# The tanh of the second MoE's up projection goes to a PSUM bank, half a block at a time

## Chip, cores and metric

One NeuronCore of a Trainium2 chip runs the whole program. The metric is device time in microseconds (us), the median of three runs; lower is better.

## What is computed

```python
kv = einsum('bhsd,bhse->bhde', k, v); out = einsum('bhsd,bhde->bhse', q, kv)      # 8 x 8 heads, 576 x 64
x  = out / sqrt(mean(out*out, -1) + 1e-06) * g_norm                               # 4608 tokens x 512
h  = x @ w_in;   x = maximum(0.01 * h, h) @ w_out                                 # first MoE, d_ff 2048
h  = x @ w_in2;  out = (h - tanh(h)) @ w_out2                                     # second MoE, d_ff 2048
```

All inputs and the output are float32; the weights are read as raw 64-bit words and converted on the chip. The line that matters here is the last one: `h - tanh(h)`.

## The kernel before

After the attention the program has four phases, one for each weight matrix. In the trace of before, phase three (the second up projection with `h - tanh(h)`) runs on TensorE from 823.85 to 1158.70 us, and phase four (the second down projection) from there to the end.

**Blocks and products.** Phase three has 72 blocks: 9 superblocks of 512 tokens by 8 pieces of d_ff. A block is a 2 x 2 matrix of 128 x 256 tiles and is computed with seven products instead of eight (Strassen's scheme); every product is six fp16 matmuls of 128 x 256 (high and low halves of the operands). `up` (line 748) issues the products in *rounds* of seven in the order of `ORDER2`: 1 of block n, 7 and 5 of block n-1, 3 of block n-2, 6 of block n, 4 of block n-1, 2 of block n. Products 1, 6, 7, 4 of a block add up in one PSUM bank (`ps_a`), and between them ScalarE copies the bank out (`keep`, line 698): `c` after product 1, `u` after 6, `u` after 7, and the block's tile 21 (`g`) after 4. Product 6 of a block must wait for its `c`, 7 for the first `u`, 4 for the second: TensorE waits there if ScalarE is late. Products 2, 5 and 3 go to banks `ps_b` and `ps_c`, and VectorE adds them to `c` and `u` (`add`, line 707) into the 128 x 1024 tile `g`.

**The activation.** When product 3 of a block is done, `finish` starts a chain of steps: ScalarE takes the tanh of the whole `g` (128 x 1024) into a tile `th` of the pool of 21 large SBUF places (line 1428), VectorE subtracts it in two halves of 128 x 512 (line 1432), and a DMA stores `g`, which phase four reads later.

**What else runs beside it in phase three.** VectorE and ScalarE convert the last weight matrix (lines 432 to 456; later lines 518 and 521) and split the next superblock's input (lines 578 and 585, with sums on GpSimd, line 616). From about 1100 us on they make the operands of phase four (`gl`).

**What sets the order.** Nothing is scheduled on the chip. `Plan` lays all instructions on one time axis with fixed costs per step (the first numbers in the tuples, in us) and emits them in that order; each engine then runs its own instructions strictly in that order and waits on semaphores. A chain puts each step at the first gap of its engine, where a last number in a tuple allows it to overlap its successor by so much; a step that raises `NoRoom` is tried again 0.4 us later. `bank(n, ...)` marks a PSUM bank as used until `free(n)`.

**Banks.** In phase three `banks2` gives `ps_a` banks 0, 1, 4, `ps_b` 2 and 5, `ps_c` 3 and 6, so bank 7 stands idle. In phase four `ps_d`, the target of product 4, has bank 4 for one half of the tokens and bank 7 for the other.

Of the kernel before, what the change touches and what calls it, by code (L numbers as in the profile page):

```python
# [11 lines left out]
F32 = mybir.dt.float32  # L12
I32 = mybir.dt.int32
AF = mybir.ActivationFunctionType
ALU = mybir.AluOpType
# [15 lines left out]
P = 128  # L31
# [172 lines left out]
@with_exitstack  # L204
def body(ctx, tc, *args):
    q, out, w1 = args[0], args[-1], args[4]
    sizes = (*q.shape, *out.shape, w1.shape[1])
    pools = {
        "const": ctx.enter_context(tc.tile_pool(name="const", bufs=1)),
        "wpool": ctx.enter_context(tc.tile_pool(name="wpool", bufs=1)),  # L210
        "work": ctx.enter_context(tc.tile_pool(name="work", bufs=1)),
        "dram": ctx.enter_context(tc.tile_pool(name="dram", bufs=1, space=DRAM)),
        "ps": ctx.enter_context(tc.tile_pool(name="ps", bufs=1, space=PSUM)),
    }
    delays = {}
    unseen = Unseen()
    while True:
        late = lay_out(Plan(delays, True), unseen, {n: unseen for n in pools}, sizes, [unseen] * len(args))
        if late is None:
            break  # L220
        delays[late[0]] = delays.get(late[0], 0.0) + late[1]
    with tc.manual_schedule():
        lay_out(Plan(delays, False), tc.nc, pools, sizes, args)


def lay_out(plan, nc, pools, sizes, args):
    q, k, v, g_norm, w1, w2, w3, w4, out = args
# [6 lines left out]
    T2 = 256  # L234
# [8 lines left out]
    L, M, X = (Slots(plan, work, kind, n) for kind, n in (("l", NL), ("m", NM), ("x", NX)))  # L243
    at = plan.at

    used = set()

    def bank(n, name):
        if n in used:
            plan.miss(("bank", n))  # L250
        used.add(n)
        return ps.tile([P, 512], F32, tag=f"p{n}", name=name)

    def free(n):
        used.discard(n)
        plan.met(("bank", n))
# [902 lines left out]
    t = 1.0  # L1159
# [7 lines left out]
    for o in order:  # L1167
        if o[0] == "a":
            held = {}
# [52 lines left out]
    for hp in range(4):  # L1222
        c = PAIRS[hp]
        t_, held = ta[0, c]
# [16 lines left out]
    for b in range(1, B):  # L1241
        for hp in range(4):
# [4 lines left out]
            held = ta[b, c][1] if (b, c) in ta else {}  # L1247
# [172 lines left out]
    spread(lambda i, kk, t: split_late(2, i, kk, t, L, M), UNITS, end1 + 45.0, end2 - 28.0)  # L1420


    def tanh(g, s):
        held = {}

        def one():
            held["t"] = L.take([P, 4, T2], F32, "th", True)
            nc.scalar.activation(out=held["t"].ap, in_=g(), func=AF.Tanh)  # L1428

        def two(n):  # L1430
            o = g()[:, 2 * n:2 * n + 2]
            nc.vector.tensor_tensor(out=o, in0=o, in1=held["t"].ap[:, 2 * n:2 * n + 2], op=ALU.subtract)  # L1432

        return [
            ("A", 1.15, one),
            ("V", 0.7, lambda: two(0)), ("V", 0.7, lambda: two(1)),
            (None, 0.0, lambda: L.give(held["t"])),
        ]

    def banks2(n):  # L1440
# [7 lines left out]

    state["rest"] = second_scales(whole, NS2, end2 + 12.0)
    up(1, T2, NS2, x1ops, tanh, lambda s: consts[s][1:3], banks2, ORDER2, between2, freed_to(3, 0.4))  # L1450
    end3 = plan.pe
    c3 = end2 + 0.45 * (end3 - end2)
# [77 lines left out]
```

## Time and profile before

| | |
|---|---|
| median of 3 runs | 1490.52 us (1490.04 to 1491.99) |
| profiled execution, its own time | 1495.29 us |
| its span (first to last instruction) | 1493.5 us |
| granted TensorE clock, mean | 0.986 of full speed (1.00 throughout phases two to four) |
| busy: TensorE, VectorE, ScalarE, GpSimd | 97%, 83%, 63%, 40% of the span |

The profiled execution is 4.8 us longer than the median, of which 1.8 us lie outside its span. TensorE is busy nearly throughout, so what matters is not the busy share of another engine but the places where TensorE waits for one.

### The profile page before, as it was taken

Reading aid. Unit: us, or ns where it says so; the run is one execution under the profiler, and the core shown is the slowest. Engines: PE = TensorE matmul, PEld = TensorE weight load, DVE = VectorE, ACT = ScalarE, POOL = GpSimd, SP = SyncE. Lnnn points to the kernel's source line nnn. Section 1 sums busy time; section 2 is a strip of 40 time slices with the busy share of each in tenths; the row PEclk is TensorE's granted clock in tenths of the full one; section 3 lists DMA queues with packets and bytes.
Section 4 is the critical chain, followed back from the end, with each engine's and each line's share of the span. In section 5 each row is a group of like instructions: output and inputs, shape, how many; then the busy total and the mean of one; then the engine's idle time right before and its main releaser. Section 6 shows DMA issues by size and latency. Waiting matters only on the chain. (4 is left out here: it accounts for less than half of the span.)

```text
span 1493.5 us, 32922 instructions
## 1 busy us (share of the span) xinstructions
PE 1443.8 (97%) x12674; PEld 1195.8 (80%) x12674; DVE 1245.4 (83%) x2029; ACT 933.7 (63%) x1529; POOL 599.8 (40%) x614
## 2 busy tenths in 40 slices
PE   5699999999999999999999999999999999999998
PEld 3467777767777777777777888888888888888887
DVE  4896687677877899999996999989999998888871
ACT  5587777778877644444542677768888555555540
POOL 3141340453643444445542111126577444444430
PEclk8799999999999999999999999999999999999999
DMA  9737898899978745555555856646678744444421
GB/s 281 182 105 228 267 298 263 275 327 306 335 260 300 296 166 191 173 173 200 178 172 198 307 211 221 209 172 221 250 253 320 282 143 154 142 143 146 150 86 36
DMA packets 156461, 321.83 MB, mean 215 GB/s; under 512 B 16656, under 2 KB 98448, under 8 KB 156304
## 3 DMA queue, kind: packets, MB, share of 16 engines
q1 hardware_dynamic: 156304, 319.73, 64.7%
q8 instruction: 99, 1.62, 0.4%
q14 instruction: 58, 0.48, 0.1%
HBM read 189.66 MB, written 130.01 MB: 214 GB/s over the span
## 5 line engine op out<-in xcount | busy, mean ns | idle before, releaser
L639 PEld LDWEIGHTS <-w 128*128 128x128 f16 x8400 | 820.1, 98 | 198.1 <-issue 19.2
L616 POOL TENSOR_TENSOR gl<-gl 128x256 f32<-128x256 f32 (+1 forms) x288 | 322.9, 1122 | 368.3 <-DVE gl L616 132.4
L639 PE MATMUL ps_a<-ops,w 128*128 128x288 f16 (+1 forms) x2400 | 331.7, 282 | 6.5 <-ACT c L696 2.8
L639 PE MATMUL ps_c<-ops,w 128*128 128x288 f16 (+1 forms) x2352 | 314.7, 282 | 2.4 <-DVE g L707 2.3
L639 PE MATMUL ps_a<-opa,w 128*128 128x288 f16 (+1 forms) x2016 | 284.6, 281 | 5.6 <-DVE w L521 4.1
L639 PEld LDWEIGHTS <-ops 128*128 128x128 f16 x1728 | 169.1, 98 | 20.0 <-issue 0.4
L639 PE MATMUL ps_b<-opa,w 128*128 128x288 f16 (+1 forms) x1200 | 175.5, 283 | 0.2 <-DVE r_w L344 0.2
L616 DVE TENSOR_TENSOR gl<-gl 128x288 f32<-128x288 f32 (+1 forms) x256 | 142.4, 558 | 4.3
L616 POOL TENSOR_TENSOR x1g<-x1g 128x256 f32<-128x256 f32 x72 | 69.5, 966 | 172.0 <-PE ps_a L639 109.9
L639 PEld LDWEIGHTS <-opa 128*128 128x128 f16 x1296 | 126.8, 98 | 14.7
L576 ACT ACTIVATE ops<-gl 128x1152 f16<-128x1152 f32 x64 | 74.3, 1161 | 96.2 <-POOL gl L616 96.0
L585 DVE SCALAR_TENSOR_TENSOR ops<-gl,inv,ops 128x1024 f16<-128x1024 f32 x72 | 104.3, 1450 | 28.1 <-ACT ops L578 28.0
L578 ACT ACTIVATE ops<-gl,inv 128x1024 f16<-128x1024 f32 x72 | 82.3, 1144 | 65.7 <-POOL gl L616 65.7
L1432 DVE TENSOR_TENSOR g<-g,th 128x512 f32<-128x512 f32 x144 | 111.9, 787 | 0.9 <-ACT th L1428 0.9
L698 ACT ACTIVATE u<-ps_a,up 128x256 f32<-128x256 f32 x144 | 68.1, 473 | 55.0 <-PE ps_a L639 51.3
L583 DVE TENSOR_TENSOR ops<-gl,ops 128x1152 f16<-128x1152 f32 x64 | 94.2, 1475 | 6.9 <-ACT ops L576 6.9
L707 DVE SCALAR_TENSOR_TENSOR g<-ps_c,u 128x288 f32<-128x288 f32 x128 | 57.9, 452 | 49.2 <-PE ps_c L639 48.5
L639 PE MATMUL ps_c<-w,ops 128*128 128x256 f16 x864 | 97.3, 273 | 0.2 <-DVE osb L707 0.2
L639 PE MATMUL ps_a<-w,ops 128*128 128x256 f16 x864 | 95.8, 273 | 0.0
L1079 POOL TENSOR_TENSOR xg<-xg,bc 128x288 f32<-128x288 f32 x48 | 44.8, 961 | 123.8 <-DMA bc<-iv 55.1
L583 DVE TENSOR_TENSOR opa<-gl,opa 128x864 f16<-128x864 f32 x64 | 81.0, 1266 | 2.0 <-ACT opa L576 1.6
L585 DVE SCALAR_TENSOR_TENSOR opa<-gl,inv,opa 128x768 f16<-128x768 f32 x72 | 79.6, 1106 | 0.8 <-ACT opa L578 0.8
(133 smaller groups left out, 2062.3 us busy)
## 6 DMA issues: line engine op xcount, KB each, us to landing
g<-g SPq DMA_DIRECT2D x64, 576.0 KB, 5.1
gl<-g SPq DMA_DIRECT2D x64, 576.0 KB, 4.5
g<-g SPq DMA_DIRECT2D x72, 512.0 KB, 3.4
gl<-g SPq DMA_DIRECT2D x72, 512.0 KB, 4.2
wd<-wo SPq DMA_DIRECT2D x48, 448.0 KB, 3.4
w<-wd SPq DMA_DIRECT2D x24, 896.0 KB, 8.5
words<-in_moe_w_in_dram SPq DMA_DIRECT2D x64, 256.0 KB, 7.1
words<-in_moe_w_out_dram SPq DMA_DIRECT2D x64, 256.0 KB, 4.5
```

The lines of the kernel that those rows point to most:

```text
L576: nc.scalar.activation(out=o, in_=i_, func=AF.Copy)
L578: nc.scalar.activation(out=o, in_=i_, func=AF.Identity, scale=scale())
L583: nc.vector.tensor_tensor(out=o, in0=i_, in1=h, op=ALU.subtract)
L585: nc.vector.scalar_tensor_tensor(out=o, in0=i_, scalar=scale(), in1=h, op0=ALU.mult, op1=ALU.subtract)
L616: lambda: e.tensor_tensor(out=g()[:, o], in0=g()[:, a], in1=g()[:, b], op=op),
L639: nc.tensor.matmul(out=out_, lhsT=a, rhs=c, start=start and m == 0, stop=stop and m == n - 1, skip_group_check=not fresh,)
L698: nc.scalar.activation(out=t, in_=src, func=AF.Identity, scale=self.scale)
L707: nc.vector.scalar_tensor_tensor(out=o, in0=src, scalar=self.minus if sub else self.scale, in1=t, op0=ALU.mult, op1=ALU.add,)
L1079: e.tensor_tensor(out=x, in0=x, in1=held[kk].ap[:, n0:n1], op=ALU.mult)
L1432: nc.vector.tensor_tensor(out=o, in0=o, in1=held["t"].ap[:, 2 * n:2 * n + 2], op=ALU.subtract)
```

## The change

The tanh is taken half a block at a time into PSUM bank 7 (a bank holds just 128 x 512 float32), and VectorE subtracts it from there. The second half can only be written once the first has been subtracted, since there is one such bank for the whole phase; so can the first half of the next block. The large SBUF place for `th` is gone.

```diff
+    TANH = 7
+
     def tanh(g, s):
         held = {}
 
-        def one():
-            held["t"] = L.take([P, 4, T2], F32, "th", True)
-            nc.scalar.activation(out=held["t"].ap, in_=g(), func=AF.Tanh)
+        def one(n):
+            if TANH in used:
+                raise NoRoom("bank")
+            held[n] = bank(TANH, "th")[:, :2 * T2].rearrange("p (o t) -> p o t", o=2)
+            nc.scalar.activation(out=held[n], in_=g()[:, 2 * n:2 * n + 2], func=AF.Tanh)
 
         def two(n):
             o = g()[:, 2 * n:2 * n + 2]
-            nc.vector.tensor_tensor(out=o, in0=o, in1=held["t"].ap[:, 2 * n:2 * n + 2], op=ALU.subtract)
+            nc.vector.tensor_tensor(out=o, in0=o, in1=held[n], op=ALU.subtract)
+            free(TANH)
 
         return [
-            ("A", 1.15, one),
-            ("V", 0.7, lambda: two(0)), ("V", 0.7, lambda: two(1)),
-            (None, 0.0, lambda: L.give(held["t"])),
+            step for n in range(2)
+            for step in (("A", 0.65, lambda n=n: one(n), 0.5), ("V", 0.65, lambda n=n: two(n), 0.4))
         ]
```

The lines after it move down by four (1436 is the subtraction now, 1432 the tanh). Because the steps cost the plan something else, the order around them changes too. TensorE's order stays the same but for two tiny matmuls of a weight's scale.

**ScalarE, one round in the middle of phase three** (the round that begins at 922.69 us in the trace of before; `c1`, `u3`, `u2`, `g` are the copies out of `ps_a` after products 1, 7, 6, 4, `unit` is a weight conversion). Before:

```order
L698 ACTIVATE c1_12352<-ps_a_12335,up0_10543 128x256 [waits PE_49]
L698 ACTIVATE u3_12367<-ps_a_12271,up0_10543 128x256 [waits PE_49]
L432 ACTIVATE unit_12379<-words_12190 128x512 [waits DMAHW6_49,DMAHW5_49]
L698 ACTIVATE u2_12395<-ps_a_12335,up0_10543 128x256 [waits PE_49]
L698 ACTIVATE g_12342<-ps_a_12271,up0_10543 128x256 [waits PE_49]
L1428 ACTIVATE th_12407<-g_12278 128x1024 [waits DVE_49,Activation_49]
```

and now:

```order
L1432 ACTIVATE th_12369<-g_12245 128x512 [waits DVE_49]
L698 ACTIVATE c1_12387<-ps_a_12371,up0_10543 128x256 [waits PE_49]
L1432 ACTIVATE th_12402<-g_12178 128x512 [waits DVE_49]
L698 ACTIVATE u3_12404<-ps_a_12302,up0_10543 128x256 [waits PE_49]
L432 ACTIVATE unit_12417<-words_12221 128x512 [waits DMAHW5_49,DMAHW4_49]
L1432 ACTIVATE th_12433<-g_12245 128x512 [waits DVE_49]
L698 ACTIVATE u2_12435<-ps_a_12371,up0_10543 128x256 [waits PE_49]
L698 ACTIVATE g_12378<-ps_a_12302,up0_10543 128x256 [waits PE_49]
```

The tanh stood behind the four copies of its round; now one half stands ahead of `u3` and one ahead of `u2`, and both wait for VectorE.

**VectorE, the same round, now** (`ps_b` and `ps_c` rows are the additions of line 707; a row that reads `th` is the subtraction):

```order
L707 SCALAR_TENSOR_TENSOR g_12378<-ps_b_12361,up0_10543,c1_12320 128x256 [waits DMAHW4_49,PE_49]
L456 SCALAR_TENSOR_TENSOR unit_12235<-words_12031,unit_12235 128x512 [waits DVE_49]
L1436 TENSOR_TENSOR g_12245<-g_12245,th_12369 128x512 [waits Activation_49]
L707 SCALAR_TENSOR_TENSOR g_12378<-ps_c_12395,up0_10543,u3_12404 128x256 [waits PE_49,Activation_49]
L707 SCALAR_TENSOR_TENSOR g_12309<-ps_c_12323,up0_10543,u2_12291 128x256 [waits PE_49]
L1436 TENSOR_TENSOR g_12178<-g_12178,th_12402 128x512
L436 TENSOR_SCALAR unit_12417,mw_325<-unit_12417 128x512 [waits Activation_49]
```

The half `th_12369` is subtracted behind a weight conversion, and `th_12402` behind the two additions of this round, the first of which needs `u3_12404`.

**VectorE at the passage from phase three to phase four, now** (the last additions of phase three, then operands of phase four, `ops`, `opa`, `gl`):

```order
L585 SCALAR_TENSOR_TENSOR ops_16013<-gl_15763,inv0_10540,ops_16013 128x1024 [waits DMAHW2_49,Pool_49]
L1436 TENSOR_TENSOR g_15877<-g_15877,th_16045 128x512 [waits Activation_49]
L707 SCALAR_TENSOR_TENSOR g_16021<-ps_c_16026,up7_11125,u2_15998 128x256 [waits PE_49]
L585 SCALAR_TENSOR_TENSOR opa_16041<-gl_15927,inv0_10540,opa_16041 128x768 [waits DMAHW0_49]
L1436 TENSOR_TENSOR g_15952<-g_15952,th_16064 128x512 [waits Activation_49]
L616 TENSOR_TENSOR gl_15927<-gl_15927 128x256 [waits DVE_49]
```

The fourth matmul into `ps_d`, the first one into bank 7, has a new wait on VectorE: for the subtraction of `th_16064`. The last three halves no longer stand here. They come some 25 VectorE instructions later, behind the two additions that read `ps_d` in phase four's first superblock, once bank 7 is free again.

## Rows read from the trace of the kernel before

**Rows 1.** The page: busy time and share of the span, instructions, of each engine.

```profile
PE 1443.8 (97%) x12674; PEld 1195.8 (80%) x12674; DVE 1245.4 (83%) x2029; ACT 933.7 (63%) x1529; POOL 599.8 (40%) x614
```

**Rows 2.** Waits of TensorE in phase three: us in total, times, longest.

```profile
PE ps_c L639 <- DVE g L707: 1.9, 2, 1.5
PE ps_a L639 <- ACT c L698: 0.6, 1, 0.6
PE ps_a L639 <- DVE r_w L344: 0.5, 1, 0.5
```

**Rows 3.** Groups of phase three by shape: names, shapes, count | busy us, mean ns | idle before.

```profile
L1432 DVE TENSOR_TENSOR g<-g,th 128x512 f32<-128x512 f32 x144 | 111.9, 787 | 0.9 <-ACT th L1428 0.9
...
L1428 ACT ACTIVATE th<-g 128x1024 f32<-128x1024 f32 x72 | 75.3, 1048 | 1.5 <-DVE g L707 1.4
...
L707 DVE SCALAR_TENSOR_TENSOR g<-ps_c,up,u 128x256 f32<-128x256 f32 x144 | 65.9, 477 | 13.2 <-PE ps_c L639 9.8
...
L456 DVE SCALAR_TENSOR_TENSOR unit<-words,unit 128x512 int32<-128x512 int32 x13 | 8.8, 680 | 0.0
...
L432 ACT ACTIVATE unit<-words 128x512 f32<-128x512 f32 x13 | 8.7, 670 | 0.0
...
L616 DVE TENSOR_TENSOR gl<-gl 128x256 f32<-128x256 f32 x3 | 1.2, 410 | 0.0
...
L711 DVE TENSOR_TENSOR xst<-u,ps_d 128x288 f32<-128x288 f32 x2 | 0.9, 444 | 0.0
```

**Rows 4.** The tile `th`, the subtractions: ns min/median/max.

```profile
L1432 DVE TENSOR_TENSOR g<-g,th x144: 669/684/1268, 839.5 to 1169.6; 128x512 f32<-128x512 f32 x144
```

**Rows 5.** Timeline: VectorE beside GpSimd: start us, us, engine, line, op.

```profile
906.33 3.86 POOL L616 TENSOR_TENSOR x1g<-x1g 128x256 f32<-128x256 f32 x4 [1.20 <-ACT u L698]
906.46 1.21 DVE L1432 TENSOR_TENSOR g<-g,th 128x512 f32<-128x512 f32 x1
...
907.59 0.86 DVE L707 SCALAR_TENSOR_TENSOR g<-ps_c,up,u 128x256 f32<-128x256 f32 x2
```

**Rows 6.** Timeline: one round of phase three, from product 1 on.

```profile
922.69 0.82 PE L639 MATMUL ps_a<-opa,w 128*128 128x256 f16 x6
922.89 0.48 DVE L707 SCALAR_TENSOR_TENSOR g<-ps_b,up,c 128x256 f32<-128x256 f32 x1
...
924.20 0.47 ACT L698 ACTIVATE u<-ps_a,up 128x256 f32<-128x256 f32 x1 [0.18 <-PE ps_a L639]
...
924.93 1.07 DVE L707 SCALAR_TENSOR_TENSOR g<-ps_c,up,u 128x256 f32<-128x256 f32 x2 [0.35 <-PE ps_c L639]
925.31 0.82 PE L639 MATMUL ps_a<-ops,w 128*128 128x256 f16 x6
...
925.97 0.82 PE L639 MATMUL ps_a<-opa,w 128*128 128x256 f16 x6
926.17 0.47 ACT L698 ACTIVATE u<-ps_a,up 128x256 f32<-128x256 f32 x1 [0.93 <-PE ps_a L639]
...
927.93 0.82 PE L639 MATMUL ps_a<-ops,w 128*128 128x256 f16 x6
```

**Rows 7.** Windows late in phase three: us, busy (x) of each engine, PEclk, DMA, GB/s.

```profile
1100.00:1135.00 35.00, 35.00 (x323) 31.36 (x322) 34.80 (x47) 30.54 (x50) 28.24 (x27) 1.00 0.70 251
1135.00:1170.00 35.00, 33.06 (x302) 29.24 (x300) 35.00 (x52) 25.80 (x37) 18.05 (x16) 1.00 0.99 369
```

**Rows 8.** Timeline: end of phase three and start of phase four (at 1158.70).

```profile
1155.51 1.47 PE L639 MATMUL ps_c<-ops,w 128*128 128x256 f16 x12 [1.52 <-DVE g L707]
...
1157.53 0.86 DVE L707 SCALAR_TENSOR_TENSOR g<-ps_c,up,u 128x256 f32<-128x256 f32 x2
...
1158.45 1.06 ACT L1428 ACTIVATE th<-g 128x1024 f32<-128x1024 f32 x1 [0.30 <-DVE g L707]
...
1160.01 0.82 PE L639 MATMUL ps_d<-w,opa 128*128 128x256 f16 x6
...
1165.09 1.28 DVE L1432 TENSOR_TENSOR g<-g,th 128x512 f32<-128x512 f32 x2
```

## The prediction, made before the changed kernel was run

> **What bounds the kernel now.** I read the page first: TensorE is busy 1443.8 of 1493.5 us [rows 1], so the other engines count only where TensorE waits for them. The change touches phase three alone (823.85 to 1158.70 us), so its waits come next: 1.9 us for VectorE's additions, 0.6 for a copy, 0.5 for a weight's scale, 3.0 us in all [rows 2]. In phase four nothing of note is left to win. **So the change can gain 3 us at the very most**, which is 0.2% of 1490.5 us (3.0 us), about what a measurement of this kernel can tell from no change. What it can lose is not bounded so.
>
> How near TensorE is to waiting shows in one round [rows 6]. Counted from product 1 at 922.69: the second copy `u` (after product 7) starts at 1.51 and ends at 1.98, and product 4, which needs it, starts at 3.28; the copy after product 6 starts at 3.48, ends at 3.95, and product 7 of the next round needs it at 5.24 (927.93). ScalarE has 1.3 us of slack at each. VectorE's first addition starts at 0.20, the pair of `ps_c` at 2.24 and 2.83. VectorE, in contrast, falls behind: in the two windows from 1100 to 1170 it is busy 34.80 and 35.00 of 35 us [rows 7], and the largest wait of phase three, 1.52 us at 1155.51, is for it [rows 8]. That its lateness costs so little is due to `th`: with 21 large places ScalarE can write a tanh while VectorE has not subtracted the one before. Just that is what the change takes away.
>
> **The parts, one by one.**
>
> *VectorE's subtractions* stay 144 of 128 x 512. Their mean is 787 ns, their median 684, the longest 1268 [rows 3, 4]: beside GpSimd's sums one took 1.21 us, while two additions with an operand in PSUM took 0.86 us together beside the same sums, no more than their usual 477 each (the second starts 0.09 before the first ends) [rows 3, 5]. With `th` in PSUM I take 0.68 throughout: a `TENSOR_TENSOR` took 410 ns for 256 elements from SBUF and 444 for 288 with one operand in PSUM, 34 ns for 32 elements more [rows 3], so PSUM costs nothing extra there, and 224 further elements at the same slope give 0.68. That is 144 x (0.787 - 0.68) = 15 us less for VectorE, most of it beside GpSimd. Of it only what shortens a wait counts: at most the 1.9 us, and I credit them in full, as VectorE is freed in just these windows.
>
> [...]
>
> *ScalarE's tanh*: 72 of 1.048 us become 144 of half the size. No row shows ScalarE writing PSUM; a pass over 128 x 512 into SBUF took 0.67 [rows 3], and I take that. Below: 0.38, if only the slope of these two rows is left, (1.048 - 0.670)/512 = 0.74 ns per element. Above: 0.96, if the fixed 0.29 came twice (the worked round below would then lose 1.0 instead of 0.42). ScalarE gets 144 x 0.67 - 75.3 = 21 us more in 335 us, at 30.5 of 35 us in its fullest window [rows 7]; as load it fits.
>
> *The wait for the one bank* is the new thing. Each half now runs tanh, subtraction, tanh, subtraction in turn on two engines that also serve TensorE, in fixed order, with a hand-over of 0.06 us (an addition ended at 1158.39, the tanh began at 1158.45 [rows 8]). Back to back on one engine I let the next start 0.09 before the last ends, as above. The round whose orders stand above is the tightest that repeats, so I work it out, from its product 1: VectorE adds at 0.20, converts (0.68 [rows 3]) from 0.59, subtracts `th_12369` from 1.18 to 1.86. Only then may `th_12402` start: 1.92 to 2.59. `u3`, behind it, runs 2.50 to 2.97 instead of 1.51 to 1.98, still before 3.28. The conversion follows from 2.88 to 3.55. VectorE's pair of additions needs `u3`, so it runs from 3.03 and 3.42 to 3.90, the subtraction of `th_12402` from 3.81 to 4.49, `th_12433` from 4.55 to 5.22, and `u2`, queued behind it, from 5.13 to 5.60. With the hand-over that is 5.66, where product 7 wanted it at 5.24: **TensorE waits 0.42 us**. The same pattern (a tanh ahead of `u3`, another pass, a tanh ahead of `u2`) stands in five of the 72 rounds: 5 x 0.42 = 2.1 us. In the others no tanh, or only one, stands before a copy with work behind it, and by the same working 0.15 to 0.3 us of the 1.3 us of slack are left.
>
> That rest is used up where VectorE is late beside GpSimd, once per superblock. A two-SBUF operation there took about 0.5 us longer (1.21 against 0.68); with three such in a row ahead of a subtraction, 1.5 us, of which the idle time of the next round takes back about 1, I put 0.2 us beyond the slack on each of eight passages: 1.6 us, an estimate.
>
> *The passage to phase four.* The first matmul into bank 7 there is the fourth into `ps_d`, 0.33 us after 1160.01 [rows 8]. It now waits for `th_16064`, whose subtraction stands behind an addition, an operand of 128 x 768 and another subtraction. In before the corresponding subtraction was one of the pair that ended at 1166.37 [rows 8], 6 us too late; the new order puts less ahead of it. Counted from TensorE's arrival: the subtraction before it ends about when phase four begins, then tanh 0.67, subtraction 0.68, two hand-overs and about 1.5 us of operand work, 3.0 us, against 1.6 us until the matmul is due. I take 1.5 us; the ends are 0 and 6.
>
> *Edits at nothing.* The last three halves run in phase four: three tanh and three subtractions there (4 us) beside engines that are not waited for; bank 7 is next wanted a superblock later, and the `g` they complete only in the last one. The store of `g` and its place in SyncE's queue move by a few rows; nobody waits for it before phase four. The freed SBUF place and GpSimd's shifted sums have no reader that TensorE waits for. If that cover failed, each would show as a wait of TensorE on `opa` or `ops`.
>
> **Sum**: -1.9 + 2.1 + 1.6 + 1.5 = +3.3 us. Against the profiled execution 1495.3 + 3.3 = 1498.6; the runs lie 4.8 us below it, so the median goes from 1490.5 to **1493.8 us**.
>
> **The rivals.**
>
> *A. The wait is hidden and nothing else changes.* For: the worked wait is 0.42 us behind two tanh; at 0.46 instead of 0.67 each it is gone, and everywhere else there is slack. Then -1.9 + 1.5 = 1490.1 us, and without a wait at the passage 1488.6. This is the rival on the other side, not slower; it decides if a half tanh into PSUM takes under 0.46 us, which lies between my ends. Against: the hand-overs alone are four per block, and the order leaves little.
>
> *B. VectorE's lateness passes to TensorE in the last third.* From 1030 us on there are 28 rounds, GpSimd is busy up to 28 of 35 us [rows 7], and where it sat beside a subtraction it will sit beside another two-SBUF operation. If each of these rounds loses the 0.42 us, that is 28 x 0.42 = 11.8 in place of 1.6 of the terms above: -1.9 + 2.1 + 11.8 + 1.5 = +13.5, 1504 us. For: VectorE has no idle time there at all. Against: up to 15 us less to do.
>
> [...]
>
> *D. More than 3 us faster*: there is no such wait to remove in this phase [rows 2]; only an effect outside it could do that.
>
> **How the numbers follow.** My forecast (1491.5 to 1497) 0.43, A 0.36, B 0.13, C 0.05, D 0.03. The bound of 3.0 us lies at 1493.5: of the forecast's case a little over half is above it, with B and C 0.43 slower; A and the rest of the forecast 0.53 the same; 0.04 faster. The range for 8 in 10 leaves out D, a little of A's best end and the far half of B: 1488.6 to 1501.0; the likeliest case alone is 1491.5 to 1497.
>
> **What would show it.** In the changed profile: the subtraction's mean near 680 ns with a maximum under 800; the tanh at 0.67 (under 0.46 speaks for A); new waits of TensorE `ps_a` on ScalarE's `u` in rounds like the worked one, some 0.4 us each, a superblock (36.7 us) apart; the 1.52 us at 1155 gone and a wait of `ps_d` on the subtraction in its place; in B dense waits of 0.3 us and more from 1030 us on. The forecast is wrong if TensorE's waits in phase three stay under 3 us or exceed 12, or if waits appear in phase four.

## The result, and the profile after

The changed kernel takes 1501.19 us (median of 4 runs, 1500.12 to 1503.27) against 1491.26 for before (4 runs, 1490.04 to 1493.81): ratio 1.0066, 95% interval 1.0047 to 1.0085. It is slower by 10 us, three times the forecast and 0.2 us beyond the upper end of the range.

The page and the waits of TensorE from 824 to 1175 us; they answer to [rows 1, 2] (engine, tile and line that waited, what it waited for, us in total, times, longest).

```profile
PE 1441.2 (96%) x12674; PEld 1192.5 (79%) x12674; DVE 1224.4 (82%) x2029; ACT 935.5 (62%) x1601; POOL 571.7 (38%) x614
```

```profile
PE ps_a L639 <- ACT c L698: 4.3, 10, 0.8
PE ps_a L639 <- ACT u L698: 3.0, 6, 1.1
PE ps_d L639 <- DVE g L1436: 1.5, 1, 1.5
```

VectorE has 21 us less to do and TensorE's work is unchanged. The 1.9 us behind VectorE's additions are gone; 7.3 us behind ScalarE's copies, where before had 0.6, and 1.5 us at the passage have come.

A stop costs more than the idle time in such a row. A matmul is shown with 0.27 us, but in a full row the next one starts 0.109 us after it, so a stop is measured here from start to start: that distance less 0.109. The phases are measured in the same way: phase three from the start of its first matmul to the start of phase four's first, phase four from there to the end of the last matmul (us).

| | before | after | difference |
|---|---|---|---|
| phase three | 334.85 | 342.78 | +7.93 |
| phase four | 330.69 | 332.37 | +1.68 |

The tile `th` in the trace of after, which answers to [rows 4] (ns min/median/max), and the two windows of [rows 7] (busy us and instructions of PE, PEld, DVE, ACT, POOL, then PEclk, DMA, GB/s).

```profile
L1432 ACT ACTIVATE th<-g x144: 587/602/627, 834.1 to 1198.4; 128x512 f32<-128x512 f32 x144
L1436 DVE TENSOR_TENSOR g<-g,th x144: 667/678/689, 834.8 to 1200.0; 128x512 f32<-128x512 f32 x144
```

```profile
1100.00:1135.00 35.00, 33.99 (x307) 29.80 (x305) 32.41 (x51) 31.04 (x58) 18.01 (x22) 1.00 0.72 249
1135.00:1170.00 35.00, 31.09 (x280) 27.14 (x278) 29.53 (x48) 26.09 (x48) 13.04 (x17) 1.00 0.96 344
```

The subtraction no longer has a slow case beside GpSimd (maximum 689 ns, 1268 before), and VectorE is no longer full in either window. TensorE nevertheless lost a microsecond in the first.

One of the larger stops of phase three, in the timeline of after (start us, us, engine, line, op; in brackets the idle time before and what ended it).

```profile
1135.94 0.60 ACT L1432 ACTIVATE th<-g 128x512 f32<-128x512 f32 x1 [0.94 <-DVE g L1436]
...
1136.48 0.46 ACT L698 ACTIVATE g<-ps_a,up 128x256 f32<-128x256 f32 x1
1136.58 0.69 DVE L1436 TENSOR_TENSOR g<-g,th 128x512 f32<-128x512 f32 x1 [0.67 <-ACT th L1432]
...
1137.30 0.60 ACT L1432 ACTIVATE th<-g 128x512 f32<-128x512 f32 x1 [0.36 <-DVE g L1436]
...
1137.83 1.13 ACT L578 ACTIVATE ops<-gl,inv 128x1024 f16<-128x1024 f32 x1
...
1138.87 0.45 ACT L698 ACTIVATE c<-ps_a,up 128x256 f32<-128x256 f32 x1
...
1139.38 0.81 PE L639 MATMUL ps_a<-ops,w 128*128 128x256 f16 x6 [0.83 <-ACT c L698]
```

Product 6 wants `c` at 1138.4 and gets it at 1139.38. ScalarE stood idle twice for the bank (0.94 and 0.36 us) and then made an operand, and `c` had its place in the order behind all of it. ScalarE was not overloaded; it was held.

### The profile page after: what moved, and what is told of

Same layout as the page of the kernel before. It is cut to its first block, busy times and chain, and to the rows that moved or that the text cites. A ratio compares the mean times of both kernels' runs of the same rounds, so it can differ in the third digit from the quotient of the medians.

```text
span 1501.5 us, 32864 instructions
## 1 busy us (share of the span) xinstructions
PE 1441.2 (96%) x12674; PEld 1192.5 (79%) x12674; DVE 1224.4 (82%) x2029; ACT 935.5 (62%) x1601; POOL 571.7 (38%) x614
## 5 line engine op out<-in xcount | busy, mean ns | idle before, releaser
L616 POOL TENSOR_TENSOR gl<-gl 128x256 f32<-128x256 f32 (+1 forms) x288 | 311.7, 1083 | 388.1 <-DVE gl L616 149.0
L616 POOL TENSOR_TENSOR x1g<-x1g 128x256 f32<-128x256 f32 x72 | 58.3, 811 | 178.8 <-DVE opa L585 162.6
L1432 ACT ACTIVATE th<-g 128x512 f32<-128x512 f32 x144 | 86.5, 600 | 50.4 <-DVE g L1436 50.1
L1436 DVE TENSOR_TENSOR g<-g,th 128x512 f32<-128x512 f32 x144 | 97.8, 679 | 12.4 <-ACT th L1432 12.3
L707 DVE SCALAR_TENSOR_TENSOR g<-ps_c,up,u 128x256 f32<-128x256 f32 x144 | 65.2, 479 | 24.1 <-ACT u L698 11.4
```

What stands on the lines that cost most here:

```text
L616: lambda: e.tensor_tensor(out=g()[:, o], in0=g()[:, a], in1=g()[:, b], op=op),
L707: nc.vector.scalar_tensor_tensor(out=o, in0=src, scalar=self.minus if sub else self.scale, in1=t, op0=ALU.mult, op1=ALU.add,)
L1432: nc.scalar.activation(out=held[n], in_=g()[:, 2 * n:2 * n + 2], func=AF.Tanh)
L1436: nc.vector.tensor_tensor(out=o, in0=o, in1=held[n], op=ALU.subtract)
```

## The experiments

All kernels are variants of the changed one; there is no e6. Phase lengths are from each one's profile, as above; ratios are to before, timed in the same session. The ratios agree with the phase lengths within 2.1 us everywhere, so I argue from the lengths. Each length is that of a single profile; the changed kernel's two profiles agree within 0.05 us. The diffs show the lines that matter, and `...` stands for what goes with them, such as giving a place back.

| kernel | phase three | phase four | ratio, 95% interval |
|---|---|---|---|
| before | 334.85 | 330.69 | 1 |
| after | 342.78 | 332.37 | 1.0066 (1.0047 to 1.0085) |
| e1, halves in many SBUF places | 336.62 | 332.67 | 1.0027 (1.0013 to 1.0040) |
| e2, halves in one SBUF place | 354.40 | 333.13 | 1.0150 (1.0124 to 1.0177) |
| e3, two banks in turn | 334.63 | 333.02 | 1.0024 (1.0007 to 1.0041) |
| e4, last three blocks in SBUF | 342.09 | 331.42 | 1.0067 (1.0044 to 1.0089) |
| e5, bank marked free late | 334.17 | 332.53 | 1.0010 (0.9998 to 1.0022) |
| e7, e3 with the second tanh ahead | 336.96 | 333.30 | 1.0030 (1.0017 to 1.0044) |
| e8, e1 with the second tanh ahead | 336.14 | 335.26 | 1.0046 (1.0029 to 1.0063) |
| e9, usual overlaps in the plan | 337.84 | 356.37 | 1.0183 (1.0160 to 1.0206) |
| e10, e5 with `ps_d` later | 334.17 | 334.27 | 1.0025 (1.0014 to 1.0036) |
| e11, e5 with e4 | 334.26 | 332.27 | 1.0012 (0.9996 to 1.0029) |
| e12, e2 marked free late | 345.57 | 335.07 | 1.0098 (1.0077 to 1.0120) |
| after again | 342.83 | 332.36 | 1.0060 (1.0041 to 1.0078) |

The theories: **one place** (a single bank makes ScalarE wait for VectorE, and copies wait behind it), **load** (two passes of ScalarE for one), **PSUM** (its access is dear), and, once the first four runs were in, **order** against **scarcity**: is it that the plan puts the tanh too early, or that one place can't be handed over fast enough in any order?

### Which part of the change: e1 to e4

e1 keeps the halves and drops the bank:

```diff
-            held[n] = bank(TANH, "th")[:, :2 * T2].rearrange("p (o t) -> p o t", o=2)
+            if n == 0:
+                held["t"] = L.take([P, 4, T2], F32, "th", True)
+            held[n] = held["t"].ap[:, 2 * n:2 * n + 2]
...
```

> The tanh still runs by half blocks, but into one of the many large places of SBUF; only the one bank is gone from the change. If the one place is the cause (a tanh waits for the subtraction of the one before, and the copies queued behind it are late): TensorE's waits in phase three fall from 8.8 us to about 3, the wait at the passage to phase four (1.5 us) goes, and the time is that of before within 1.5 us, 1490 to 1492.5. If the load of two passes in place of one is the cause: a half into SBUF takes 0.67 us, 144 x 0.67 = 96 us, 10 us more than the 87 us of the changed kernel, so the waits behind ScalarE stay or grow and the time stays at 1499 us or above. If writing and reading PSUM is the cause, it is also the time of before, so this run doesn't part these two; the next one does.

e2 keeps the one place and puts it in SBUF, which leaves 20 large places instead of 21:

```diff
-            held[n] = bank(TANH, "th")[:, :2 * T2].rearrange("p (o t) -> p o t", o=2)
+            used.add(TANH)
+            held[n] = const.tile([P, 2, T2], F32, tag="th", name="th")
...
```

> The opposite part alone: one single half place as in the change, but in SBUF instead of PSUM (the large places become 20 instead of 21 to make room). If the one place is the cause: the waits of TensorE in phase three are there again, and more of them, since a half tanh takes 0.67 us instead of 0.60 and a subtraction beside GpSimd up to 1.2 instead of 0.69: 9 to 20 us of waits, 1501 to 1512 us. If PSUM itself is the cause, the time is near before's, 1490 to 1494.

The tile `th` in e1, then TensorE's waits in its phase three; the same two views of e2.

```profile
L1432 ACT ACTIVATE th<-g x144: 612/620/657, 832.8 to 1161.0; 128x512 f32<-128x512 f32 x144
L1436 DVE TENSOR_TENSOR g<-g,th x144: 670/684/1232, 833.5 to 1163.7; 128x512 f32<-128x512 f32 x144
```

```profile
PE ps_a L639 <- ACT u L698: 1.4, 2, 0.8
PE ps_c L639 <- DVE g L707: 1.0, 3, 0.5
PE ps_a L639 <- ACT c L698: 0.3, 1, 0.3
```

```profile
L1437 DVE TENSOR_TENSOR g<-g,th x144: 673/686/1251, 832.6 to 1181.6; 128x512 f32<-128x512 f32 x144
```

```profile
PE ps_a L639 <- ACT c L698: 10.8, 12, 2.0
PE ps_a L639 <- ACT u L698: 6.3, 13, 1.1
```

With many places the waits are 2.7 us, with one they are 17.1. So the loss hangs on the one place, not on load or PSUM: e1 carries more tanh load than after (0.620 us a half against 0.602), and in the same one-place scheme PSUM is 11.6 us better than SBUF (354.40 - 342.78). e1 was expected at the time of before and is 3.8 us longer: 1.8 in phase three, and 2.0 at the passage, where a copy of phase four now waits. That part of the expectation failed. e2 lost what was expected of one place, in time (ratio 1.0150, some 22 us) a little more.

e3 gives the tanh two banks, at the expense of `ps_b`:

```diff
-    TANH = 7
+    TANH = (7, 5)
...
-        return dict(a=(0, 1, 4)[n % 3], b=(2, 5)[n % 2], c=(3, 6)[n % 2])
+        return dict(a=(0, 1, 4)[n % 3], b=2, c=(3, 6)[n % 2])
```

> The change with two banks in turn: bank 5 is taken from ps_b (which keeps bank 2 alone) and given to the tanh. If the one place is the cause, a tanh then waits only for the subtraction of the half before last: the waits behind ScalarE's copies in phase three fall from 7.3 us to under 2, that at the passage falls or goes, and the time is 1490 to 1494; the risk is the single ps_b, whose addition has one round's time (4.6 us) before the bank is written again. If the load of the two passes or the use of PSUM is the cause, the time stays at 1499 or above.

Phase three is that of before (334.63). The passage is worse, as bank 5 is `ps_b`'s in phase four and wanted earlier than bank 7; the timeline of e3 shows it.

```profile
1161.56 1.28 DVE L1438 TENSOR_TENSOR g<-g,th 128x512 f32<-128x512 f32 x2
1162.29 0.49 PE L639 MATMUL ps_b<-w,opa 128*128 128x256 f16 x3 [2.16 <-DVE g L1438]
```

e4 sends the tanh of the last three blocks to the large places:

```diff
+            if whole_:
+                if n == 0:
+                    held["t"] = L.take([P, 4, T2], F32, "th", True)
+                held[n] = held["t"].ap[:, 2 * n:2 * n + 2]
+                nc.scalar.activation(out=held[n], in_=g()[:, 2 * n:2 * n + 2], func=AF.Tanh)
+                return
...
```

> The change, but the last three blocks' tanh goes to the large places of SBUF, so that bank 7 is free when phase four begins. If the wait of ps_d there costs what its row shows, 1.5 us (1.7 us by the length of phase four), the time falls by about 1.6 us from the changed kernel's 1501.2 to 1499.6, and the waits of phase three before its last three blocks stay as they are, 7 us. If the last blocks' single place also delays the copies there (waits at 1154 and 1163 us), up to 1 us more is won: 1498.6. If the wait at the passage is hidden elsewhere later, nothing changes.

The 1.5 us wait of `ps_d` is gone; TensorE's waits from 1164 to 1182 us in e4:

```profile
PE ps_a L639 <- ACT c L698: 0.6, 1, 0.6
```

By the lengths it gains 1.6 us as expected (0.7 in phase three, 0.95 in phase four). The timed ratios show none of it (1.0067 for e4, 1.0066 and 1.0060 for after), but their intervals are too wide to tell so little.

### Order or scarcity: e5, e9, e12

In the change `free(TANH)` runs where the plan *starts* the subtraction. The plan may therefore give the bank to the next tanh at once, some 0.7 us before it can really be had, and emit that tanh ahead of copies. e5 changes one line:

```diff
-            free(TANH)
+            at(plan.now + 0.75, lambda: free(TANH))
```

> The changed kernel, but its plan marks bank 7 free 0.75 us after the place where it puts the subtraction (about when the subtraction really ends) instead of at its start, so that the next half tanh is put into ScalarE's order later, behind copies that stood behind it. Theory order: a tanh stands in ScalarE's order before the bank can be free, and the copies behind it stand still with it. Then the waits behind copies fall from 7.3 us to under 2.5, phase three from 342.8 us (the start of its first matmul to that of phase four's first) to 335 to 338, the time to 1.001 to 1.004 of before's; the wait at the passage stays or grows, since the tanh are later still. Theory scarcity: one place can't hand over fast enough whatever the order, so the waits stay at 7 us or more, phase three at 341 or above, and the time at 1.006 or above.

TensorE's waits in phase three of e5, then ScalarE's wait for the bank there, then the same row of after (824 to 1165).

```profile
PE ps_a L639 <- ACT c L698: 1.0, 3, 0.6
PE ps_a L639 <- ACT u L698: 0.6, 2, 0.4
```

```profile
ACT th L1432 <- DVE g L1436: 23.3, 35, 2.8
```

```profile
ACT th L1432 <- DVE g L1436: 47.2, 70, 3.0
```

Still one bank, but TensorE's waits fall from 7.3 us to 1.6 and ScalarE stands before the bank 35 times instead of 70. Phase three is 8.6 us shorter than after's and 0.7 shorter than before's. **Order, not scarcity, made the loss in phase three.** The timeline of e5 at the same product (block 67, product 6; the stop of 0.99 us shown above):

```profile
1129.26 0.67 DVE L1436 TENSOR_TENSOR g<-g,th 128x512 f32<-128x512 f32 x1
...
1130.03 0.60 ACT L1432 ACTIVATE th<-g 128x512 f32<-128x512 f32 x1 [0.29 <-DVE g L1436]
...
1130.56 0.46 ACT L698 ACTIVATE g<-ps_a,up 128x256 f32<-128x256 f32 x1
...
1130.92 0.47 ACT L698 ACTIVATE c<-ps_a,up 128x256 f32<-128x256 f32 x1
...
1132.27 0.60 ACT L1432 ACTIVATE th<-g 128x512 f32<-128x512 f32 x1 [0.31 <-DVE g L1436]
1132.60 0.82 PE L639 MATMUL ps_a<-ops,w 128*128 128x256 f16 x6
```

Here one half, and neither the second nor an operand, stands between the subtraction and `c`; the second half comes behind `c` and waits where nothing is behind it that TensorE wants soon; `c` is there 1.2 us before product 6. Over all rounds, a half stands ahead of the first copy `u` in 14 rounds of after and in 5 of e5. The line moves rows on every engine, so which of the moves saved which stop is not shown one by one; that the mark in the plan is the cause is. Of the stops, those in the first superblock stay (837 to 845 us, 1.6 us in three); the first two of them, 0.55 and 0.40, stand in e1 too and so don't come from the bank; before has the second alone (0.41 at 840.81).

e12 is e2 with the same line.

> One half place in SBUF (as in the run that was 22 us slower than before), with the place marked free late. If the order alone made those 17.8 us of phase three over the run with many places, phase three falls from 354.4 to 336 to 338 us, as with the bank in PSUM. If the order only costs much where one place is slow to hand over (a subtraction beside GpSimd takes up to 1.25 us from SBUF, more than the 0.75 us that the plan now allows), phase three stays above 340.

TensorE's waits in phase three of e12:

```profile
PE ps_a L639 <- ACT c L698: 5.0, 8, 1.5
PE ps_a L639 <- ACT u L698: 4.3, 9, 1.0
```

The late mark takes 8.8 us of e2's phase three (354.40 to 345.57), but 345.57 is far above e5's 334.17. Between e5 and e12 only the memory of the one place differs (and one large place, 20 for 21): 0.75 us covers a subtraction of at most 0.69, not one that takes up to 1.25 beside GpSimd, as in e2. The expectation's second case came true. So order counts in SBUF too. That the 11.4 us left between e12 and e5 come from the slow hand-over fits these numbers but is not shown: no run marks the place in SBUF free later still.

> The changed kernel without its two overlap numbers (0.5 and 0.4 us, by which a step may be squeezed into the plan before a step that is already there); the plan's usual 0.325 us for a step of 0.65 stands in their place, so that tanh and subtractions are squeezed in ahead of copies less often. Theory order: fewer tanh stand ahead of copies too early, the waits behind copies fall from 7.3 us to 4 to 6 and phase three from 342.8 to 339 to 341. Theory scarcity: subtractions are put later, the bank is held longer, and phase three grows or stays, 342 to 346 us.

```diff
-            for step in (("A", 0.65, lambda n=n: one(n), 0.5), ("V", 0.65, lambda n=n: two(n), 0.4))
+            for step in (("A", 0.65, lambda n=n: one(n)), ("V", 0.65, lambda n=n: two(n)))
```

e9 is inconclusive: the plan came out otherwise at many places. TensorE's waits from 1140 to 1230 us in e9, and its window at the end of phase three:

```profile
PE ps_a L639 <- ACT opa L578: 14.4, 1, 14.4
PE ps_d L639 <- DVE g L1436: 4.4, 1, 4.4
PE ps_a L639 <- ACT u L698: 2.5, 1, 2.5
```

```profile
1157.00:1162.00 5.00, 4.93 (x31) 3.74 (x31) 3.11 (x5) 2.17 (x5) 0.00 (x0) 0.66 0.81 303
```

Its six stops over 0.1 us from 990 to 1142 us sum to 1.5 us, where after loses 7.4 in fourteen up to 1145, which speaks for order. But then phase four waits 4.4 us for bank 7 and 14.4 for an operand, so the run as a whole says nothing on either theory.

### The passage, and the search for a kernel that beats both: e7, e8, e10, e11

e7 and e8 let the second half tanh run beside the first subtraction (in e3 and in e1):

```diff
-            step for n in range(2)
-            for step in (("A", 0.65, lambda n=n: one(n), 0.5), ("V", 0.65, lambda n=n: two(n), 0.4))
+            ("A", 0.65, lambda: one(0), 0.5),
+            [("V", 0.65, lambda: two(0), 0.4), ("A", 0.65, lambda: one(1), 0.5)],
+            ("V", 0.65, lambda: two(1), 0.4),
```

> Two banks in turn, as in the earlier run with two, and the second half tanh of a block may now run beside the first subtraction instead of after it. The chain of a block is 0.6 to 0.7 us shorter, so the wait at the passage to phase four (2.2 us for the subtraction that reads bank 5) falls to about 1.5, phase three stays near 334.6 us, and the ratio falls from 1.0024 to 1.001 to 1.002. If two tanh in a row delay copies instead, waits behind copies appear in phase three and it lengthens by 1 us or more. Faster than before by more than 0.2% is expected by neither.

> Halves in a large place of SBUF, as in the first run, with the second half tanh free to run beside the first subtraction. The first run was 3.8 us longer than before by its phases (1.8 us in phase three, 2.0 at the passage). If that comes from the longer chain of a block (tanh, subtraction, tanh, subtraction in turn, so that the last blocks end later and the loads behind their stores start later), it shrinks here to 1 to 2 us, ratio 1.001 to 1.0015. If it comes from ScalarE's load (90 us in place of 75), it stays at 3 us or more, ratio 1.002 to 1.003.

In neither did the shorter chain help. e7's wait at the passage stayed at 2.2 us and phase three grew by 2.3, most of it in new waits behind copies, as the second case of its expectation has it. e8's phase three shrank by 0.5 only and its passage grew by 2.6; its ratio, 1.0046, lies above both of its cases. The passage shows why: TensorE waits there 2.9 us for `c` instead of 1.5 (an operand in front of `c` waits 5.57 us for its load), and after that its matmuls start some 0.21 us apart for 3.0 us, in place of 0.109, which costs another 1.5 us. What e1's 3.8 us come from stays open: in phase three the shorter chain takes back 0.5 of 1.8 us, and at the passage the late load hides what it does.

e10 is e5 with the first two operands of phase four in another order: products 1 and 2 (into `ps_a` and `ps_b`) of both come first, and then product 4 (into `ps_d`) of both. e11 is e4 with e5's line. The edit of e10 beside that line:

```diff
-            in_turn((1, 2, 4) if s == 0 else (2, 4), then=lambda j, e: give("A", j, e))
+            if s == 0 and blk == 1:
+                for ps, js in (((1, 2), (0, 1)), ((4,), (0, 1)), ((1, 2, 4), range(2, NP))):
+                    for j in js:
+                        for p in ps:
+                            for t in range(2):
+                                e = whole(p, t, [j], s)
...
```

> The kernel with the bank marked free late, and phase four's first superblock in another order: for the first two operands the products into ps_a, ps_b and ps_c's partners come first and the two products into ps_d (the second of which takes bank 7) behind them, 2.6 us later than now. If the wait at the passage (1.5 us by its row, 1.84 us by phase four's length, 332.53 against 330.69) is only the last half tanh's bank, it goes: phase four 330.6 to 331.2 us, and the time is that of before, ratio 0.999 to 1.001. If the second operand isn't ready so early, or the copies behind the operands are late then, a wait of TensorE for an operand or a copy takes its place and phase four stays at 332 us or above. Faster than before by more than 0.2% is expected by neither: phase three has only 0.7 us less than before.

> The kernel with the bank marked free late, and the last three blocks' tanh in the large places of SBUF. Phase three stays at 334 us; the wait of 1.5 us for bank 7 goes, but with halves in SBUF a copy of phase four waited behind operand passes instead (0.6 and 1.6 us in the two earlier runs), so phase four is expected at 331 to 332.3 us and the ratio at 0.999 to 1.001. If phase four stays at 332.5 or above, moving the last tanh is no cure for the passage.

TensorE's wait at the passage of e10, and the timeline of e11 there:

```profile
PE ps_d L639 <- DVE g L1445: 3.4, 1, 3.4
```

```profile
1172.14 0.94 ACT L578 ACTIVATE opa<-gl,inv 128x768 f16<-128x768 f32 x1 [3.05 <-DMA gl<-g]
...
1172.98 1.13 ACT L578 ACTIVATE ops<-gl,inv 128x1024 f16<-128x1024 f32 x1
...
1174.03 0.81 ACT L698 ACTIVATE c<-ps_a,kap 128x256 f32<-128x256 f32 x2
...
1174.53 0.71 PE L639 MATMUL ps_a<-w,ops 128*128 128x256 f16 x5 [1.42 <-ACT c L698]
```

In e10 `ps_d` asks for bank 7 later, and the plan gives the bank to two more halves first: the wait is 3.4 us instead of 1.5, which neither case of its expectation had. In e11 the bank is free, but two operand passes stand ahead of `c`, and the first waits 3.05 us for its load; phase four comes out at the upper end of what was expected. Neither is a cure. No kernel is faster than before: the intervals of the best, e5 and e11, contain 1, and by the lengths they lie 1.2 and 1.0 us above it.

The changed kernel ran once more beside e10 to e12:

> The changed kernel as it is, on the same chip as the three others: phase three 342.8 us, ratio to before 1.005 to 1.008. It gives the difference to the kernel with the late mark on one chip.

It repeats itself (342.83 us, ratio 1.0060), and its interval lies wholly above that of e5.

## Why the prediction was wrong, and where it was right

The direction of the sum, the worked round and the passage came as forecast, though the chances gave "the same" 0.53 and "slower" 0.43. The loss was three times the sum because one term, the wait in all the other rounds, was put at 1.6 us and measured 6.8, with 1.5 more in the first superblock.

**The bound held.** No kernel of this study gains 3 us in phase three; the best is 0.7 us below before. (Counted from start to start, before's four waits there cost 3.6 us, not 3.0.)

**The subtractions**: 0.68 us was forecast, 0.678 measured, maximum 0.689. That PSUM costs a subtraction nothing extra held: the median is 678 ns with `th`, one of the two operands, in PSUM, and 684 with it in SBUF (e1). The stalls of 1155 and 1158 us are gone: term -1.9, by starts (1.69 + 0.58) -2.3.

**The tanh**: 0.67 taken, 0.602 measured. Its price alone put rival A out: it needed 0.46. Only 0.018 us of the difference is PSUM's (e1 has 0.620); the row I took it from was a pass of another kind. ScalarE got 11 us more, not 21.

**The worked round** came out as worked. Timeline of after, the round that was worked out:

```profile
926.51 0.68 DVE L1436 TENSOR_TENSOR g<-g,th 128x512 f32<-128x512 f32 x1
...
927.22 0.60 ACT L1432 ACTIVATE th<-g 128x512 f32<-128x512 f32 x1 [0.98 <-DVE g L1436]
...
927.36 0.82 PE L639 MATMUL ps_a<-opa,w 128*128 128x256 f16 x6
...
927.76 0.46 ACT L698 ACTIVATE u<-ps_a,up 128x256 f32<-128x256 f32 x1
...
928.26 0.60 PE L639 MATMUL ps_a<-ops,w 128*128 128x256 f16 x4
```

Subtraction, tanh, copy, product 7, as forecast; the product should start at 927.36 + 6 x 0.109 = 928.01 and starts 0.25 us late. Two tanh of 0.60 for 0.67 take 0.14 off my 0.42, which leaves 0.28. Its twins at 891.34 and 965.20 lose 0.25 as well; the two in rounds 43 and 62 lose 1.27 (already at product 4, which waits for the first `u`) and 0.57. Together 2.6 us for the term of 2.1. The trace has the pattern in a sixth round, 53, which loses 0.10.

**The passage**: 1.5 forecast, 1.51 in the row of `ps_d` and 1.68 by the length of phase four, by the chain that was named, though its parts came out otherwise:

```profile
1165.66 0.68 DVE L1436 TENSOR_TENSOR g<-g,th 128x512 f32<-128x512 f32 x1
...
1166.38 0.60 ACT L1432 ACTIVATE th<-g 128x512 f32<-128x512 f32 x1 [1.02 <-DVE g L1436]
1166.65 1.01 DVE L585 SCALAR_TENSOR_TENSOR opa<-gl,inv,opa 128x768 f16<-128x768 f32 x1
...
1167.58 0.68 DVE L1436 TENSOR_TENSOR g<-g,th 128x512 f32<-128x512 f32 x1
...
1168.32 0.49 PE L639 MATMUL ps_d<-w,opa 128*128 128x256 f16 x3 [1.51 <-DVE g L1436]
```

The subtraction before it was to end when phase four begins (1165.00 us) and ends 1.34 us later, at 1166.34; VectorE's other work between the two subtractions was to add 1.5 us and adds 0.60, since half of it runs beside the tanh. The two errors nearly cancel, so the mechanism was right and the close size was luck.

**The step that failed** is the third term, 1.6 us for eight passages of 0.2, with the sentence it rests on: that in the other rounds "no tanh, or only one, stands before a copy with work behind it", and 0.15 to 0.3 us of slack are left. From 993 us on 13 further stops of 0.13 to 0.99 us sum to 6.8 us, and four stops in the first superblock (836 to 848), for which there was no term, cost 2.0 where before lost 0.5 (0.4 us of that difference stand in e1 too and are not the bank's). Nine of the 13, 5.4 us, are stops of product 6, which waits for `c`. The prediction worked out the slack of the two copies `u` and not that of `c`, and ahead of these nine `c` stand two halves, or a half and a weight or operand. With the parts that were right: +1.5 + 2.6 + 6.8 - 2.9 (before's other seven stops of 3.5 us, less 0.6 of such stops in after) = +8.0 in phase three, where the lengths say +7.9, and +1.7 at the passage. The sign that the prediction named for its own failure, waits in phase three of under 3 or over 12 us, did not show (7.3 us in the rows): it was too wide to catch a term of this size.

I had given the reason as VectorE's lateness beside GpSimd. The windows above contradict it for the stops from 1100 us on: VectorE has 2.6 and 5.5 us of idle time in 35, and no subtraction is slowed. At the largest stop (1.27 us, round 43) it had a part: there VectorE is busy 4.97 of the 5 us from 1019.6 on, a weight conversion beside GpSimd takes 1.52 us where the median is 1.14, and the subtraction stands behind an operand. But e5 has the same passes, with that conversion at 1.43 us, and no stop, because there the first `u` of the round stands ahead of the tanh. The reason is the mark in the plan: a tanh is emitted when the bank is not yet free, waits, and holds the copies, in any round where another pass follows it. One round was worked and the slack of the rest taken from it; the rounds after 990 us, where ScalarE's passes for weights and operands fall in the same place (1137.83 above), needed the same working.

**Rival B** had the size nearly right (1504) for the wrong reason: from 1025 us on the stops sum to 7.6 us instead of 11.8, and, but for a part of the stop in round 43, not because of VectorE's load. **C**, 0.05 of the chances, had the subtraction dearer with `th` in PSUM; no run shows that, as the medians are 678 ns in PSUM and 684 in SBUF (e1). **The edits at nothing** held in after: phase four has no new stop but that of `ps_d`. In e1, e8 and e11 the passage became dear by an operand's load, so that cover is thin.

## What to carry to other kernels

In a kernel whose order is fixed beforehand, mark a shared buffer free when its last reader *ends*, not when it starts: the same single bank cost 7.9 us of phase three with the early mark and gained 0.7 with the late one. When a buffer is cut from many to one, work the hand-over through every round in which something else stands behind the waiting instruction, not through the tightest repeating one alone. And before that, ask what the change can win: here at most 3 us against a loss with no such bound.

## What was not expected of the hardware

A half tanh into PSUM took 602 ns and into SBUF 620 (e1), the same operation and shape; the gain of PSUM for the subtraction is that it isn't slowed beside GpSimd (at most 689 ns against 1232 in e1). After the 2.5 us wait in e9 TensorE's granted clock fell: its window above shows 0.66 on average, where 1140 to 1157 us had 1.00, and from 1157.1 to 1160.4 us matmuls started some 0.21 us apart in place of 0.109. Stretches of 3.0 and 3.4 us at the same spacing follow the waits of 2.9 us in e8 (1173.3 to 1176.3 us) and of 2.6 us in e12 (1184.9 to 1188.3 us). The 3.4 us wait of e10 and the 2.3 us wait at the passage of e2 were followed by none; what decides it is not shown here. In e8 and e12 the slower stretch cost some 1.5 us on top of the wait.
